# A three-step integer conversion moved from SBUF to PSUM, and slot stores that no longer wait for one another

## The chip, the cores and the metric
The kernel runs on one core of a Trainium2 chip. The number is the time of one execution in device microseconds. A core has TensorE (PE; its weight loads are shown as PEld), VectorE (DVE), ScalarE (ACT), GpSimd (POOL) and SyncE (SP), which only starts transfers here; each takes its instructions in the order of the program and waits on semaphores. SBUF is the on-chip memory, PSUM the small memory that TensorE writes and that DVE and ACT can also read and write.

## What is computed
Attention over 4 batches and 8 heads of 576 rows, in which each row keeps its 32 largest scores; then a dense two-layer network; then a layer in which each of the 2304 tokens goes to one of eight experts. The weights `w_in` and `w_out` of the dense network arrive as 64-bit floats.

```python
scores = scale * np.matmul(q, k.transpose(0, 1, 3, 2))
kth = np.partition(scores, -32, axis=-1)[..., -32:-31]
attn = softmax(np.where(scores >= kth, scores, -1e9)); x = attn @ v
h = x @ w_in                                     # 512 -> 2048
x = (np.maximum(h, 0) + alpha * np.minimum(h, 0)) @ w_out
e = argmax(x @ w_gate + modality_bias[modality_id])   # one of 8 experts
out = gate_w * (np.maximum(x @ w1[e], 0) @ w2[e])
```

## The kernel before
**The loop.** Attention runs as 72 steps of two tiles of 128 query rows. One step puts on each engine: on TensorE the scores of the next pair into the PSUM bank pair `psS` (L453, L454); on ScalarE a copy of them to SBUF (`S`, L457), a mask `u` (L526), the exponential (L530) and a 16-bit copy `HL` (L534); on GpSimd the factors `bc` (L506), the masking (L527) and the low halves of `HL` (L538, L539); on VectorE the search for the 32 largest (L471 to L501). The search begins with three instructions on `psS` and `S` (L474), and it is L471 behind them that frees `psS` for the next scores. SP then starts a transposing transfer `PT<-HL` (L541). Six steps ahead, q, k and v of a later head pair are loaded, scaled, split into 16-bit halves (`qk`, L419 on GpSimd) and transposed (`QK<-qk`, L423 on SP). All of this is one written order per engine; nothing reorders it at run time.

**The weights.** `all_weights` spreads the 32 pieces of `w_in` and `w_out` (128 x 512 64-bit words each) over the steps before 205 us. SP loads a piece into one of five buffers `wraw`. `read(x)` turns its words into 32-bit floats on DVE in three instructions: L259 shifts the high word, L260 joins the sign bits, L261 joins the top bits of the low word. In the kernel before all three write the same SBUF tile, `f32[x]`, which lies in the space of `Wi` or `Wo`, or, for the last four pieces of each matrix, in one of four tiles `wlast`. The pieces are read up to four at a time, at the end of a step, so on DVE they stand between one step's search and the next. `square` (L266, ScalarE) takes each read piece for a norm, `high` and `low` (L271 to L282) split it later; a `wlast` tile is free again only when `low` (L280 on GpSimd, L282 on DVE) has read it.

**The expert lists.** When the rank of a token within its expert is known, `place(r)` writes the token's number and weight to its slot in the DRAM table `mapD`, by an indirect transfer that GpSimd starts (L773; 18 of them from 418 to 908 us). Two stores of one chunk are declared independent; a store of the next chunk is not, so its wait includes the landing of the store before it. The list of a block (`ids<-mapD`, L1446 for block 0, L1309 for the later units) is read by SP behind the last store.

**Around block 0.** After the last attention step the loop goes on with the dense network alone: TensorE forms `psS` (L637) and then `psX` (L686), for which ScalarE makes the high part of `g` (L672) and GpSimd the low part (L673). Into that stretch falls the end of the placing: one store of the small chunk, two of chunk 7, then block 0's list.

Of the kernel before, what the change touches and what calls it, by code (L numbers as in the profile page):

```python
# [8 lines left out]
F32 = mybir.dt.float32  # L9
# [3 lines left out]
I32 = mybir.dt.int32  # L13
I64 = mybir.dt.int64
AF = mybir.ActivationFunctionType
ALU = mybir.AluOpType
# [44 lines left out]
def tile_kernel(ctx, tc, q, k, v, w_in, w_out, alpha, mod_id, w_gate, mod_bias, w1, w2, out, dbg=None, force=False):  # L61
    nc = tc.nc
    V, A, G, T, SY = nc.vector, nc.scalar, nc.gpsimd, nc.tensor, nc.sync
# [11 lines left out]
    psX = ctx.enter_context(tc.tile_pool(name="psX", bufs=2, space=PSUM))  # L75
# [4 lines left out]
    mapD = dram.tile([SLOTS, 2], I32, name="mapD")  # L80
# [78 lines left out]
    def run(exact):  # L159
        with ExitStack() as rs:  # L160
            rc = rs.enter_context(tc.tile_pool(name="rc", bufs=1))
            flags = None if exact else rc.tile([128, 2 * 144 + NFB], BF16, name="flags")
            ohs = rc.tile([128, E], F16, name="ohs")
            G.memset(ohs, 0.0)
            mp = Rec()
            with tc.manual_schedule():
                with ExitStack() as ph:
                    blk, over = phase1(exact, ph, rc, rs, flags, ohs, mp)
                mp.B = rs.enter_context(tc.tile_pool(name="moeB", bufs=1))
                if exact:  # L170
                    moe_phase(MAXBLK, blk, mp)
                else:
                    units_phase(blk, mp, lambda: doubts(rc, flags, blk, over))
            if not exact:
                return nc.values_load(blk[0:1, 32:33], min_val=0, max_val=(2 * 144 + NFB) * 128 + MAXBLK)


    def phase1(exact, ph, rc, rs, flags, ohs, mp):
# [15 lines left out]
        def at(slot, s_, f):  # L194
            hooks[slot].setdefault(s_, []).append(f)
# [34 lines left out]
        def all_weights(words, stage):  # L230

            n = 512
# [5 lines left out]
            sc, iv, raws, f32 = {}, {}, {}, {}  # L238
# [12 lines left out]
            def read(x):  # L251

                w_, i = divmod(x, 16)
                f32[x] = W[w_][:, (i + WG) * n:(i + WG + 1) * n] if i + WG < 16 else \
                    stage.tile([128, n], F32, name="wlast", bufs=WG)
                r3 = raws.pop(x).bitcast(I32).rearrange("p (n w) -> p n w", w=2)
                lo, hi = r3[:, :, 0], r3[:, :, 1]
                t_ = f32[x].bitcast(I32)
                V.tensor_scalar(t_, hi, 5, 2, op0=ALU.logical_shift_left, op1=ALU.logical_shift_right)  # L259
                V.scalar_tensor_tensor(t_, hi, -1073741824, t_, op0=ALU.bitwise_and, op1=ALU.bitwise_or)  # L260
                V.scalar_tensor_tensor(t_, lo, 29, t_, op0=ALU.logical_shift_right, op1=ALU.bitwise_or)  # L261

            def square(x):
                w_, i = divmod(x, 16)
# [331 lines left out]
        def chunk(ci, xn, rs):  # L596
            ffn = state.ffn
            c = Rec()
            R = len(rs)
# [171 lines left out]
            def place(r):  # L771
                G.memset(spacer, 0.0)
                d_ = G.indirect_dma_start(out=mapD, out_offset=bass.IndirectOffsetOnAxis(ap=c.si[:, r:r + 1], axis=0),  # L773
                                          in_=c.tg[:, r, :], in_offset=None)
                if r:
                    tc.declare_no_dep(d_.ins, c.placed.ins, reason="other slots")
                c.placed = d_
                state.placed += 1

            def keep():  # L780
# [13 lines left out]
            def after(s_):  # L794
# [28 lines left out]
                for r in range(R):  # L823
                    at("late", s_ + GATE[2] + r, lambda r=r: place(r))
# [54 lines left out]
        state = Rec()  # L879
# [6 lines left out]
        wgroup = all_weights(words, stage)  # L886
        state.ffn = state.out = None
        state.started = state.placed = 0
        state.alone = False

        def wstep(n):
# [51 lines left out]
        def first_block(s_):  # L943

            if s_ < NIT + 4:
                return at("mid", s_ + 1, lambda: first_block(s_ + 1))
            mp.A = rs.enter_context(tc.tile_pool(name="moeA", bufs=1, side="right"))
            b0 = Rec()
            cp = bankO[:, COUNTS:COUNTS + 8]
            T.matmul(cp, ones16, ohs, start=True, stop=True)  # L950
            mx = rc.tile([128, 1], F32, name="mx0")
            ge = rc.tile([128, 8], F32, name="ge0")
            ix = rc.tile([128, 1], F32, name="ix0")
            mp.oh0 = rc.tile([128, 8], F32, name="oh0")
            mp.e0 = rc.tile([128, 1], F32, name="e0")
            blk0 = rc.tile([128, 2], I32, name="blk0")


            mp.cn = rc.tile([128, 8], I32, name="cn")
            mp.cb = [rc.tile([128, 16], F32, name=f"cb{i}") for i in range(4)]  # L960
            for t_ in mp.cb:
                G.memset(t_, 0.0)
            mp.less = rc.tile([128, 8], F32, name="less")
            mp.step = rc.tile([128, 8], F32, name="step")
            mp.base = rc.tile([128, 16], F32, name="base")
            mp.ef = rc.tile([128, 16], F32, name="ef")
            mp.cx = rc.tile([128, 16], F32, name="cx")
            mp.blk = rc.tile([128, 33], I32, name="blk")
            mp.at = rc.tile([128, 8], F32, name="at8")
            mp.part = rc.tile([128, 8], I32, name="part8")  # L970
            mp.some = rc.tile([128, 8], F32, name="some8")
            mp.few = rc.tile([128, 8], F32, name="few8")
            mp.ix = rc.tile([128, 1], F32, name="ix8")
            mp.over = rc.tile([128, 1], F32, name="over")
            V.reduce_max(mx, cp, axis=AX.X)
            V.scalar_tensor_tensor(ge, cp, mx, iota8m, op0=ALU.is_ge, op1=ALU.mult)
            V.tensor_reduce(ix, ge, axis=AX.X, op=ALU.min)
            V.tensor_scalar(mp.e0, ix, 8.0, None, op0=ALU.add)
            V.tensor_copy(blk0[:, 0:1], mp.e0)
            V.tensor_scalar(blk0[:, 1:2], mp.e0, float(CAP), None, op0=ALU.mult)  # L980
            V.tensor_scalar(mp.oh0, iota8m, ix, None, op0=ALU.is_equal)

            def prepare():
                oh0 = mp.oh0
                V.tensor_scalar(mp.less, oh0, -256.0, 255.0 if exact else 0.0, op0=ALU.mult, op1=ALU.add)
                V.tensor_scalar(mp.step, oh0, -256.0, float(CAP), op0=ALU.mult, op1=ALU.add)
                V.scalar_tensor_tensor(mp.step[:, 0:7], oh0[:, 1:8], 256.0, mp.step[:, 0:7], op0=ALU.mult, op1=ALU.add)
                if exact:
                    V.tensor_scalar(mp.base, io16[:, :, 0], oh0[:, 0:1], 256.0, op0=ALU.add, op1=ALU.mult)
                else:  # L990
                    V.tensor_scalar(mp.base, io16[:, :, 0], 2.0, oh0[:, 0:1], op0=ALU.mult, op1=ALU.add)
                    V.tensor_scalar(mp.base, mp.base, 256.0, None, op0=ALU.mult)
                    V.scalar_tensor_tensor(mp.at, oh0, 256.0, ebase, op0=ALU.mult, op1=ALU.add)

            def start():
                assert state.placed == NTILE - 2
                mp.b0 = Block(0, blk0[0:1, 0:1], blk0[0:1, 1:2], mp)
                for fp in range(4):
                    mp.b0.load(fp)

            at("late", s_, start)
            at("gap", s_ + 1, prepare)
            at("late", s_ + 1, lambda: mp.b0.gather())
            for fp in range(4):
                at("gap", s_ + 2 + fp, lambda fp=fp: mp.b0.split(fp))
            at("gap", s_ + 3, lambda: mp.b0.turn())
# [48 lines left out]
        while True:  # L1055
# [69 lines left out]
            while fpq and credit >= 1 and n_ < 2 and fpq[0][0] <= s_ and weights_for(fpq[0][2]):  # L1125
                credit -= 1
                _, c, fp = fpq.pop(0)
# [173 lines left out]
    class Unit:  # L1301


        def __init__(self, i, R, ie, ip, mp):
            self.i, self.R, self.mp = i, R, mp
            self.e = SY.value_load(ie, min_val=0, max_val=E - 1)
            pos = SY.value_load(ip, min_val=0, max_val=E * CAP)
            self.ids = small.tile([128, 4, 2], I32, name="ids4")
            SY.dma_start(self.ids[:, :R], mapD[bass.ds(pos, 128 * R), :].rearrange("(p r) o -> p r o", r=R))  # L1309
            self.raw, self.wp, self.gs = {}, {}, {}  # L1310

        def gather(self):
# [82 lines left out]
    def moe_phase(nblk, blk, mp):  # L1395
# [17 lines left out]
        for i in range(1, nblk):  # L1413
# [21 lines left out]
            o.m2(3)  # L1435
            o.store()

    class Block:


        def __init__(self, i, ie, ip, mp):
            self.i, self.mp = i, mp
            self.e = SY.value_load(ie, min_val=0, max_val=E - 1)
            pos = SY.value_load(ip, min_val=0, max_val=E * CAP)
            self.ids = small.tile([128, 2, 2], I32, name="ids")
            SY.dma_start(self.ids, mapD[bass.ds(pos, 256), :].rearrange("(p r) o -> p r o", r=2))  # L1446
            self.raw, self.wp = {}, {}
            self.gs = {}
            self.Y = None
# [116 lines left out]
```

## Time and profile before
| what | value |
|---|---|
| median of three runs | 1156.09 us (1155.61 to 1158.4) |
| the profiled execution | 1153.87 us, its span 1152.2 us |
| DVE, ACT, POOL, PE busy | 823.8, 755.2, 718.0, 845.0 us |
| L259, L260, L261 | 32 each, all before 205 us |
| L773 | 18, from 418.0 to 907.8 us |

The span is the time from the first to the last instruction in the profile; the execution's own time is 1.67 us more. Line numbers (L259) are those of the kernel before. In a row of the timeline the columns are start, duration, engine, line, operation, output `<-` inputs, shape, and in brackets the idle time before it and what ended that. A wait for several semaphores is put down to the one that came last as far as the profile shows it.

### The profile page before, as it was taken

The page shows a single profiled execution, that of the slowest core. Times are in us where ns is not written, and L with a number is a line of the kernel's source. Part 1 is how long each engine was busy: PE and PEld are TensorE (multiplying, and loading weights), DVE is VectorE, ACT ScalarE, POOL GpSimd, SP SyncE. Part 2 cuts the span into 40 slices and gives each one's busy share as a digit, 9 for nine tenths or more (in the row PEclk, how much of TensorE's full clock was granted, in tenths as well). Part 3 has the DMA queues.
Part 4 walks back from the last instruction along what each step waited for, and adds up shares of the span by engine and source line. Part 5 has one row for each costly group of instructions (what it writes and reads, how often), then busy time and mean ns, then how long its engine had stood idle before and what let it go on. Part 6 is the DMA issues. An engine that isn't in the chain of part 4 may idle for free.

```text
span 1152.2 us, 21482 instructions
## 1 busy us (share of the span) xinstructions
PE 845.0 (73%) x7100; PEld 602.6 (52%) x7100; DVE 823.8 (72%) x2813; ACT 755.2 (66%) x1276; POOL 718.0 (62%) x1106
## 2 busy tenths in 40 slices
PE   0202231347869989878787878989998899999995
PEld 0001121234536557455555555667665778888884
DVE  5788878788889999999888879994326343434342
ACT  6466696898987887878888978795324243342441
POOL 4175496899898898888788999897323220230210
PEclk9999565668899999999989999999999999999998
DMA  8969965586788577586778768765104272543320
GB/s 250 251 171 237 263 145 128 137 180 162 165 202 162 107 184 126 106 177 133 147 148 172 158 138 193 155 128 79 19 19 165 86 262 75 183 135 121 129 92 22
DMA packets 297111, 170.22 MB, mean 148 GB/s; under 512 B 245458, under 2 KB 270034, under 8 KB 296988
## 3 DMA queue, kind: packets, MB, share of 16 engines
q1 hardware_dynamic: 293212, 158.24, 59.0%
q0 software_dynamic: 3776, 10.51, 2.5%
q8 instruction: 57, 0.93, 0.4%
q14 instruction: 66, 0.54, 0.2%
HBM read 81.42 MB, written 25.94 MB: 93 GB/s over the span
## 4 chain that ended last, share of the span: by engine, by line
PE 34%; DVE 23%; POOL 15%; ACT 12%; issue 7%; DMA 6%; SPq 3%; ACTq 0%; POOLq 0%
PE psX L1363 9%; PE psS L1380 9%; PE psX L686 6%; DVE X L501 4%; DVE m L477 4%; PE psS L637 4%; POOL HL L538 4%; POOL S L527 4%; DVE F L477 3%; DMA rawk<-in_k_dram 3%; ACT S L530 2%; POOL qk L419 2%; DVE gr L665 2%; ACT HL L534 2%; PE psH L637 2%
## 5 line engine op out<-in xcount | busy, mean ns | idle before, releaser
L686 PE MATMUL psX<-Wo,g 128*128 128x512 f16 x864 | 218.6, 403 | 53.8 <-POOL g L673 39.6
L527 POOL TENSOR_TENSOR S<-u,S 128x576 f32<-128x576 bf16 x144 | 184.5, 1303 | 47.4 <-ACT u L526 47.2
L637 PEld LDWEIGHTS <-Wi 128*128 128x128 f16 x1920 | 170.8, 99 | 45.7 <-DVE gr L665 14.3
L538 POOL TENSOR_TENSOR HL<-S,HL 128x512 f16<-128x512 f32 x144 | 168.2, 1168 | 20.3 <-ACT HL L534 10.5
L453 PE MATMUL psS<-QK 128*128 128x512 f16 (+1 forms) x160 | 63.7, 436 | 142.6 <-DVE B L471 109.4
L637 PE MATMUL psH<-xT,Wi 128*128 128x256 f16 (+1 forms) x1488 | 158.2, 265 | 12.3 <-DVE gr L665 8.5
L686 PEld LDWEIGHTS <-g 128*128 128x128 f16 x864 | 82.9, 103 | 157.1 <-POOL g L673 49.2
L530 ACT ACTIVATE S<-S,bc,nb 128x576 f32<-128x576 f32 x144 | 124.0, 862 | 40.7 <-POOL S L527 40.7
L453 PEld LDWEIGHTS <-QK 128*128 128x128 f16 (+1 forms) x320 | 32.1, 109 | 203.1 <-DVE B L471 59.5
L1389 POOL DMA_INDIRECT out_dram<-o,ids x18 | 19.9, 1106 | 166.8 <-ACT o L1387 164.0
L477 DVE MAX8 m<-X 128x8 f32<-128x160 f32 x432 | 117.6, 314 | 0.0
L673 POOL TENSOR_TENSOR g<-gr,g 128x512 f16<-128x512 f32 x72 | 84.0, 1166 | 52.6 <-ACT g L672 47.3
L526 ACT ACTIVATE u<-S,bc 128x576 bf16<-128x576 f32 x144 | 103.1, 765 | 15.8 <-POOL bc L506 15.8
L1370 DVE SCALAR_TENSOR_TENSOR gl<-psX,gh 128x512 fp32r<-128x512 f32 (+1 forms) x40 | 25.4, 637 | 115.5 <-ACT gh L1369 110.9
L534 ACT ACTIVATE HL<-S 128x576 f16<-128x576 f32 x144 | 91.3, 680 | 12.9 <-DMA PT<-HL 12.7
L1369 ACT ACTIVATE gh<-psX 128x512 fp32r<-128x512 f32 (+1 forms) x40 | 22.3, 557 | 109.7 <-PE psX L1363 107.9
L457 ACT ACTIVATE S<-psS 128x576 f32<-128x576 f32 x144 | 84.1, 633 | 8.6 <-PE psS L454 8.6
L501 DVE MATCH_REPLACE8 X<-m,X 128x160 f32<-128x160 f32 x288 | 87.0, 310 | 0.0
L558 PE MATMUL bankO<-VV,PT 128*128 128x66 f16 (+1 forms) x2240 | 86.0, 200 | 0.0
L558 PEld LDWEIGHTS <-PT 128*128 128x128 f16 (+1 forms) x2240 | 82.3, 105 | 4.8 <-issue 3.5
L474 DVE SCALAR_TENSOR_TENSOR X<-psS,S 128x288 f32<-128x288 f32 (+1 forms) x144 | 80.8, 603 | 2.5
L672 ACT ACTIVATE g<-gr 128x512 f16<-128x512 f32 x72 | 44.9, 623 | 40.5 <-DVE gr L665 24.1
(290 smaller groups left out, 2098.6 us busy)
## 6 DMA issues: line engine op xcount, KB each, us to landing
raw<-in_moe_w_dram SPq DMA_DIRECT2D x40, 512.0 KB
qkD<-QK SPq DMA_DIRECT2D x16, 576.0 KB
QK<-qkD SPq DMA_DIRECT2D x16, 576.0 KB
wraw<-in_moe_w_in_dram SPq DMA_DIRECT2D x16, 512.0 KB
wraw<-in_moe_w_out_dram SPq DMA_DIRECT2D x16, 512.0 KB
vvD<-VV SPq DMA_DIRECT2D x16, 325.0 KB
VV<-vvD SPq DMA_DIRECT2D x16, 325.0 KB
K<-QK SPq DMA_DIRECT2D x32, 144.0 KB
```

What stands on the lines that cost most here:

```text
L477: ops.append(lambda: V.max(o, a_))
L501: ops.append(lambda i_=i_, r=r: V.match_replace(out=dst(i_), in_to_replace=m[:, i_, 8 * r:8 * r + 8], in_values=src(i_) if r == 0 else dst ...
L526: A.activation(u, t.S, AF.Relu, scale=-BIG, bias=t.cut)
L527: G.tensor_tensor(t.S, u, t.S, op=ALU.subtract)
L530: A.activation(t.S, t.S, AF.Exp, scale=t.c.negc, bias=t.b)
L534: A.activation(t.HL.rearrange("p a b -> p (a b)")[:, 0:S], t.S, AF.Copy)
L538: G.tensor_tensor(f[:, 640:1152], t.S[:, 0:512], f[:, 0:512], op=ALU.subtract)
L558: T.matmul(oo, l, r, start=(n_ == 0), stop=(n_ == len(ops) - 1), skip_group_check=True)
L637: T.matmul(h[:, fb, :], Wi[:, 4 * cc + f0 // 512, wh, f0 % 512:f0 % 512 + 128], c.xT[:, :R, xh_, cc, :], start=(n == 0), stop=(n == 11))
L686: T.matmul(c.X2[r], g[:, gh, fb, r * 128:r * 128 + 128], Wo[:, FB * fp + fb, wh, :], start=(fp == 0 and fb == 0 and n == 0), stop=(fp == c ...
L1363: T.matmul(h, w_[:, cc, f0:f0 + 128], x_[:, cc, :], start=(n == 0), stop=(n == 11))
L1380: T.matmul(self.Y[r], g_[:, r * 128:r * 128 + 128], w_[:, j % 2, :], start=(j == 0 and n == 0), stop=(j == 7 and n == 2))
```

## The change
Three edits. The first two results of `read` go to a PSUM tile `psX` (two buffers, which the dense network uses only later); only the third is written to SBUF. Each store of `place` is declared independent of all stores before it. In return every list read names all the stores that no list has named yet (`behind`), in place of the dependence that came through the chain of stores.

```diff
-                t_ = f32[x].bitcast(I32)
+                t_ = psX.tile([128, n], F32, name="psX").bitcast(I32)
                 V.tensor_scalar(t_, hi, 5, 2, op0=ALU.logical_shift_left, op1=ALU.logical_shift_right)
                 V.scalar_tensor_tensor(t_, hi, -1073741824, t_, op0=ALU.bitwise_and, op1=ALU.bitwise_or)
-                V.scalar_tensor_tensor(t_, lo, 29, t_, op0=ALU.logical_shift_right, op1=ALU.bitwise_or)
+                V.scalar_tensor_tensor(f32[x].bitcast(I32), lo, 29, t_, op0=ALU.logical_shift_right, op1=ALU.bitwise_or)
...
-                if r:
-                    tc.declare_no_dep(d_.ins, c.placed.ins, reason="other slots")
-                c.placed = d_
+                for p_ in state.places:
+                    tc.declare_no_dep(d_.ins, p_.ins, reason="other slots")
+                state.places.append(d_)
...
+                mp.places, mp.seen = state.places, 0
+                behind(mp.b0.list, mp)
...
+    def behind(list_, mp):
+        for p_ in mp.places[mp.seen:]:
+            tc.add_manual_dep(list_.ins, p_.ins.name, mybir.DependencyInfo(
+                mybir.DependencyClass.Sync, mybir.DependencyReason.DATA), reason="all that was placed")
+        mp.seen = len(mp.places)
```

The order of instructions on every engine is the same in both kernels; what differs is the operands and the waits. On DVE, at the start of the program (`wraw` is the loaded piece, `Wi` the SBUF tile), before:

```order
L259 TENSOR_SCALAR Wi<-wraw 128x512 [waits DMAHW7_49]
L260 SCALAR_TENSOR_TENSOR Wi<-wraw,Wi 128x512 [waits DVE_49]
L261 SCALAR_TENSOR_TENSOR Wi<-wraw,Wi 128x512 [waits DVE_49]
L259 TENSOR_SCALAR Wi<-wraw 128x512 [waits DMAHW0_49]
L260 SCALAR_TENSOR_TENSOR Wi<-wraw,Wi 128x512 [waits DVE_49]
```

and after:

```order
L259 TENSOR_SCALAR psX<-wraw 128x512 [waits DMAHW7_49]
L260 SCALAR_TENSOR_TENSOR psX<-wraw,psX 128x512 [waits DVE_49]
L261 SCALAR_TENSOR_TENSOR Wi<-wraw,psX 128x512 [waits DVE_49]
L259 TENSOR_SCALAR psX<-wraw 128x512 [waits DMAHW0_49]
L260 SCALAR_TENSOR_TENSOR psX<-wraw,psX 128x512 [waits DVE_49]
```

Only the tiles are others: L260 and L261 now have one operand in PSUM and one in SBUF. On POOL, where the small chunk's store and chunk 7's two stand one behind the other (the waits named DMASW are landings of transfers that POOL started), before:

```order
L745 COPY tg<-tok 128x2 [waits DMASW4_49,DMASW3_49]
L772 MEMSET spacer 1x1
L773 DMA mapD<-tg,si 18944x2
L772 MEMSET spacer 1x1 [waits Pool_49]
L773 DMA mapD<-tg,si 18944x2 [waits DMASW5_49,DVE_49]
L772 MEMSET spacer 1x1 [waits Pool_49]
L773 DMA mapD<-tg,si 18944x2
L673 TENSOR_TENSOR g<-gr,g 128x512 [waits Activation_49]
```

and after:

```order
L745 COPY tg<-tok 128x2 [waits DMASW4_49,DMASW3_49]
L772 MEMSET spacer 1x1
L773 DMA mapD<-tg,si 18944x2
L772 MEMSET spacer 1x1 [waits Pool_49]
L773 DMA mapD<-tg,si 18944x2 [waits DVE_49]
L772 MEMSET spacer 1x1 [waits Pool_49]
L773 DMA mapD<-tg,si 18944x2
L673 TENSOR_TENSOR g<-gr,g 128x512 [waits Activation_49]
```

The wait for one landing, DMASW5, is gone from the second store; L673, which TensorE needs, stands behind all three. On SP, at block 0's list, before:

```order
L1446 DMA ids<-mapD 128x4 [waits DMAHW5_49,DMASW7_49]
```

and after (the line is L1455 there):

```order
L1455 DMA ids<-mapD 128x4 [waits DMASW5_49,DMASW4_49,DMASW6_49,DMASW3_49,DMASW7_49,DMASW2_49,DMAHW5_49,DMASW1_49,DMASW0_49]
```

The list waits for the landings of all stores by name in place of the last one's alone.

## Rows read from the trace of the kernel before
**Rows 1.** Page, part 2: busy tenths in 40 slices of 28.8 us.
```profile
DVE  5788878788889999999888879994326343434342
POOL 4175496899898898888788999897323220230210
```
**Rows 2.** Windows, 0 to 205 us, of L259, L260, L261: length, DVE busy (count).
```profile
0.00:205.00 205.00, 22.82 (x32) 0.81 0.77 204
0.00:205.00 205.00, 28.23 (x32) 0.81 0.77 204
0.00:205.00 205.00, 29.77 (x32) 0.81 0.77 204
```
**Rows 3.** Lines one by one: ns min/median/max, first and last start, shape.
```profile
L259 DVE TENSOR_SCALAR wlast<-wraw x8: 408/1370/1642, 57.4 to 191.9; 128x512 int32<-128x512 int32 x8
L260 DVE SCALAR_TENSOR_TENSOR Wi<-wraw,Wi x12: 691/693/1639, 9.8 to 56.1; 128x512 int32<-128x512 int32 x12
L474 DVE SCALAR_TENSOR_TENSOR psS<-psS,S x72: 441/453/467, 39.8 to 776.6; 128x288 f32<-128x288 f32 x72
L1370 DVE SCALAR_TENSOR_TENSOR gl<-psX,gh x40: 408/692/693, 935.0 to 1136.1; 128x512 fp32r<-128x512 f32 x32, 128x256 fp32r<-128x256 f32 x8
L212 DVE TENSOR_SCALAR sck<-bankO x16: 150/153/154, 14.7 to 653.5; 128x3 int32<-128x3 int32 x16
```
**Rows 4.** Groups by line and shape, DVE: busy us, mean ns, idle before.
```profile
L572 DVE TENSOR_SCALAR den<-bankO,sv 128x4 f32<-128x4 f32 x32 | 8.8, 276 | 5.9 <-PE bankO L558 5.9
```
**Rows 5.** Lines one by one, POOL.
```profile
L216 POOL TENSOR_SCALAR sci<-sck x16: 227/236/692, 15.3 to 659.4; 128x3 int32<-128x3 int32 x16
L419 POOL TENSOR_TENSOR qk<-rawk,qk x16: 1267/1282/1718, 19.9 to 670.1; 128x576 f16<-128x576 f32 x16
```
**Rows 6.** Timeline, 55 to 110 us, of DVE, POOL and SP.
```profile
55.61 0.41 DVE L259 TENSOR_SCALAR Wi<-wraw 128x512 int32<-128x512 int32 x1
68.10 0.46 DVE L474 SCALAR_TENSOR_TENSOR psS<-psS,S 128x288 f32<-128x288 f32 x1
...
58.13 3.23 POOL L527 TENSOR_TENSOR S<-u,S 128x576 f32<-128x576 bf16 x2 [10.82 <-ACT u L526]
...
64.64 2.47 SPq L423 DMA_TRANSPOSE QK<-qk  x1
...
98.25 0.41 DVE L259 TENSOR_SCALAR Wo<-wraw 128x512 int32<-128x512 int32 x1
109.29 0.46 DVE L474 SCALAR_TENSOR_TENSOR psS<-psS,S 128x288 f32<-128x288 f32 x1
```
**Rows 7.** Timeline, 175 to 206 us, of DVE, PE and POOL.
```profile
179.55 1.36 DVE L259 TENSOR_SCALAR wlast<-wraw 128x512 int32<-128x512 int32 x1 [3.06 <-POOL Wi L280]
193.70 0.46 DVE L474 SCALAR_TENSOR_TENSOR psS<-psS,S 128x288 f32<-128x288 f32 x1
...
196.19 0.59 PE L453 MATMUL psS<-QK 128*128 128x512 f16 x1 [22.91 <-DVE B L471]
...
201.78 0.20 POOL L506 TENSOR_TENSOR bc<-m,nb 128x4 f32<-128x4 f32 x1 [10.34 <-DVE wp1k L212]
...
204.69 2.54 POOL L527 TENSOR_TENSOR S<-u,S 128x576 f32<-128x576 bf16 x2
```
**Rows 8.** Timeline, 860 to 870 us, of POOL, PE and SP.
```profile
860.17 0.98 POOL L773 DMA_INDIRECT mapD<-tg,si  x1 [0.42 <-issue]
864.57 0.97 POOL L773 DMA_INDIRECT mapD<-tg,si  x1 [3.32 <-DVE mx L975]
865.84 0.97 POOL L773 DMA_INDIRECT mapD<-tg,si  x1 [0.22 <-issue]
866.84 1.16 POOL L673 TENSOR_TENSOR g<-gr,g 128x512 f16<-128x512 f32 x1
...
868.05 2.33 PE L686 MATMUL psX<-Wo,g 128*128 128x512 f16 x10 [3.28 <-POOL g L673]
...
869.62 0.36 SPq L1446 DMA_DIRECT2D ids<-mapD  x1
```

More of the change, by code (lines that the diff above doesn't have):

```diff
@@ L888, in phase1 @@
         state.started = state.placed = 0
+        state.places = []
         state.alone = False
@@ L1308, in __init__ @@
             self.ids = small.tile([128, 4, 2], I32, name="ids4")
-            SY.dma_start(self.ids[:, :R], mapD[bass.ds(pos, 128 * R), :].rearrange("(p r) o -> p r o", r=R))
+            behind(SY.dma_start(self.ids[:, :R], mapD[bass.ds(pos, 128 * R), :].rearrange("(p r) o -> p r o", r=R)), mp)
             self.raw, self.wp, self.gs = {}, {}, {}
@@ L1445, in __init__ @@
             self.ids = small.tile([128, 2, 2], I32, name="ids")
-            SY.dma_start(self.ids, mapD[bass.ds(pos, 256), :].rearrange("(p r) o -> p r o", r=2))
+            self.list = SY.dma_start(self.ids, mapD[bass.ds(pos, 256), :].rearrange("(p r) o -> p r o", r=2))
+            if i:
+                behind(self.list, mp)
             self.raw, self.wp = {}, {}
```

## The prediction
> **What bounds the kernel now.** I read the page's slices first. DVE and POOL are both busy in most slices up to about 800 us and both idle much of the time behind that [rows 1], so the kernel has an attention part that runs on several engines at once and an end that runs on TensorE. The change touches one place in each: the reading of the weights, all of it before 205 us, and three slot stores near 864 us. So I looked at these two stretches in the timeline.
>
> In the first stretch the three lines of `read` take 22.82 + 28.23 + 29.77 = 80.8 us of DVE for 32 pieces, 2.53 us a piece [rows 2]. Line by line the same instruction has two durations: L260 takes 0.69 us in its median case and up to 1.64 us, L259 0.41 us at best and 1.37 us in the median of its late pieces [rows 3]. The added microsecond is about one POOL instruction, and POOL is stretched in the same places: L216 takes up to 0.69 us against a median of 0.24, L419 up to 1.72 against 1.28, both at 15 to 22 us [rows 5]. The two engines hold each other up. With the short durations a piece would cost 0.41 + 0.69 + 0.69 = 1.79 us, 57.3 us in all, so 23.5 us of the 80.8 are such waiting. L474, which reads one operand from PSUM and one from SBUF and writes PSUM, stays between 441 and 467 ns in all 72 cases, although POOL is as busy around them [rows 1, 3]. That is the form which L260 gets, and L261 gets that of L1370 (PSUM and SBUF in, SBUF out), which never exceeds 0.693 us.
>
> **The reads, price of one.** L260 and L261 go to 0.69 us each, the value of L1370 for the same 512 columns. L259 in its new form (SBUF in, PSUM out) is not in the trace. Bounds: 0.41 us if it keeps its rate, and from L474, whose 288 columns take 0.45 us, to the 0.69 us of a 512-column instruction at one column a step; L212, the same double shift on int32 with PSUM as its input, has only 0.15 us of fixed cost, so nothing more is to be expected [rows 3]. I take 0.69. A piece then takes 3 x 0.69 = 2.07 us, with the small overlap seen between pieces 2.05: a piece that POOL never held gets 0.27 us longer, a held one up to 3 us shorter. In all 32 x 2.05 = 65.6 us, 15 us less DVE. That is not the gain; it counts only where DVE ends last.
>
> [...]
>
> **Where it counts.** Place by place in the order of time:
> - 9 to 22 us. Three pieces stand ahead of the first scale factors on DVE: +0.8. Against that the POOL instructions between these and the first `QK<-qk`, which goes when L419 is done, lose what they were held for: L216 0.45 and L419 0.44 [rows 5], and of the small ones in between at least one as much, together 1.3. Net -0.5; bounds +0.8 and, with two more held alike, -1.4.
> - 55 to 68 us. Four pieces take DVE from 55.61 to 68.10, 12.5 us, which become 8.2, so -4.3 on DVE. But SP sets the pace here: its `QK<-qk` at 64.64 waits for POOL, and transfers follow it back to back. POOL's L527 pair takes 3.23 us at 58.13 against 2.54 at 204.69, where no read is about, and L419 is again up to 0.44 too long [rows 5 to 7]: with a small one -1.3. I take -1.3; bounds 0 and -4.3.
> - 98 to 109 us. Four pieces, 109.29 - 98.25 = 11.0 us, become 8.2: -2.8 [rows 6]. The transfers of SP are again dense behind it, so I take a quarter, -0.7; bounds 0 and -2.8.
> - 125 to 176 us: one piece only; ScalarE is the bound. Nothing, and if that cover is gone, 0.27.
> - 176 to 202 us. Here four pieces fill DVE from 179.55 to the search at 193.70, 14.15 us, and before them it idles 3.06 us because the `wlast` tile is still being read by POOL's L280 [rows 7]. Afterwards L259 and L260 write PSUM and need not wait for it: they run from 176.5 on (179.55 less the idle 3.06), and only L261 waits until 179.55. So the first piece ends at 180.2, the other three take 6.15 and the search begins at 186.3: -7.4. What is late next? The scores (L453 at 196.19) were waiting for L471 of that search, and the factors `bc` of POOL at 201.78, idle for 10.34 us, for the search's end [rows 7]: both follow DVE in full. POOL's L419 there is needed two steps later and ends earlier than today. Bounds: -2.8 (what POOL alone is held for there) and -7.4. I take -7.4.
>
> Sum of the reads: -0.5 - 1.3 - 0.7 - 7.4 = -9.9 us. From there to 800 us every step follows from the one before and nothing hangs on absolute time, so the shift passes through.
>
> **The stores.** POOL starts the small chunk's store at 860.17, is free of it at 861.15, and starts the next store only at 864.57, 3.4 us later, 3.32 of them idle behind the small spacer instruction. The row puts that down to L975 on DVE; but the order has no such dependence: what the store takes from DVE (its slot and weight) was ready before, and the wait that goes with the change is the landing of the store before. The list of block 0 shows a landing of that size: the last store is done at 866.81, and SP, which waits for it, starts the list at 869.62, 2.8 us later. Behind the stores on POOL stands L673, and behind that TensorE, idle for 3.28 us before 868.05 [rows 8]. Without the wait the second store starts at about 861.5, the third at 862.8, L673 runs from 863.8 to 865.0 (its input from ScalarE comes before), and TensorE goes on at about 865.05: -3.0 us. Bounds 0 and -3.3. The list goes with its last landing, some 2.5 us earlier, less than TensorE gains, but block 0's first matmul stands behind four more rounds of the dense network, so that costs nothing; if it did, 0.5 us. The other stores stand some 50 us apart from the one before; their wait was over already. The list's new waits are for landings long past, except for the last, which it waited for before; SP has nothing for TensorE queued behind it but block 0's own weights.
>
> **Sum.** -9.9 - 3.0 = -12.9 us: the profiled execution's 1153.87 becomes 1141.0. The median of the runs stands 2.2 us above that execution, so 1156.09 becomes 1143.2.
>
> **The rivals.**
> - The end of the last reads does not decide (for it: ScalarE and SP are dense up to 190 us; against: the waits of L453 and L506). Then only POOL's 2.8 us count there, and none of the small terms: -2.8 - 3.0, 1150.3.
> - The store really waited for DVE, as its row says: TensorE still stalls, -9.9 alone, 1146.2. For it: the row itself, with L975 ending just before the store; against: L975 comes later in the program than the store.
> - SP is not the bound at 55 and 98 us, and DVE's full savings count: -1.4 - 4.3 - 2.8 - 7.4 - 3.0 = -18.9, 1137.2.
> - Slower: POOL holds the new forms too. The place is DVE's reads in front of the searches. These words are read at a stride of two, which L474's are not, so its steadiness need not carry over. Then each piece keeps its waiting and pays 0.27 us for the lost rate and, if PSUM has a fixed price like that of L572 (276 ns for four columns, against 153 for L212 [rows 3, 4]), 0.12 for each of three instructions: +0.63. Eighteen pieces lie where DVE sets the pace (3, 4, 3, 4, 4, the third group behind 68 us): +11.3 - 3.0, 1164.4. It decides from the point where a piece in PSUM takes longer than the 2.53 us of today.
> - The attention part absorbs all of it, and the stores' 3.0 us are all that is left: 1153.1, which is no change that can be told.
>
> **How the numbers follow.** A difference under 0.3%, 3.5 us, can't be told from none. Chances: the forecast 0.55 (its own range 1140 to 1147), the first rival 0.15, the second 0.07, the third 0.10, the slower one 0.06, absorbed 0.07. Below 1152.6 lie the forecast and the first three, 0.87, of which I give 0.02 to no change: faster 0.85, same 0.09, slower 0.06. The range 1137.5 to 1152 leaves out the slower case, the absorbed one and about half of the third.
>
> **What would show it.** L259, L260 and L261 all near 0.69 us with no case above 0.75; the search that starts at 193.70 at about 183.8; POOL's three stores following one another within 1.3 us each, and TensorE's stall before the ten L686 down from 3.28 to about 0.3 us. Wrong would be: stretched L260 or L261; an idle DVE ahead of the search near 184; the second store still 3 us behind the first.

## The result and the profile after

The changed kernel took 1142.17 us (median of 4 runs, 1141.09 to 1143.34) against 1156.03 us before (4 runs, 1155.61 to 1158.40) on the same chip: ratio 0.9876, 95% interval 0.9859 to 0.9893. 1143.2 was predicted. On a second chip the ratio was 0.9882 (0.9857 to 0.9906). The profiled execution took 1142.26 us, 11.6 less than that of before.

The two rows of slices that answer to [rows 1], and the three windows that answer to [rows 2]:

```profile
DVE  5778778688799999999888879994225333443331
POOL 3165397899988988988788999897333220230210
```

```profile
0.00:205.00 205.00, 21.92 (x32) 0.81 0.81 212
...
0.00:205.00 205.00, 22.26 (x32) 0.81 0.81 212
...
0.00:205.00 205.00, 21.98 (x32) 0.81 0.81 212
```

The slices show little: DVE is about as busy as before (806.0 us in all, it was 823.8). The windows show that the three reads now take 66.2 us where they took 80.8; 65.6 was the estimate. Line by line (ns min/median/max, first and last start, shape), against [rows 3]:

```profile
L259 DVE TENSOR_SCALAR psX<-wraw x32: 672/685/696, 9.7 to 183.4; 128x512 int32<-128x512 int32 x32
...
L260 DVE SCALAR_TENSOR_TENSOR psX<-wraw,psX x32: 695/696/697, 10.4 to 184.1; 128x512 int32<-128x512 int32 x32
...
L261 DVE SCALAR_TENSOR_TENSOR wlast<-wraw,psX x8: 686/686/689, 59.3 to 184.8; 128x512 int32<-128x512 int32 x8
```

Not one of these instructions is stretched any more; min and max are 2 to 24 ns apart. L259, which took 0.41 us at its best, now takes 0.67 to 0.70, as priced. Now the place that carried the largest term, DVE from 175 to 186 us, which answers to [rows 7]:

```profile
175.43 0.68 DVE L259 TENSOR_SCALAR psX<-wraw 128x512 int32<-128x512 int32 x1
176.14 0.69 DVE L260 SCALAR_TENSOR_TENSOR psX<-wraw,psX 128x512 int32<-128x512 int32 x1
178.57 0.69 DVE L261 SCALAR_TENSOR_TENSOR wlast<-wraw,psX 128x512 int32<-128x512 int32 x1 [1.73 <-POOL Wi L280]
...
184.81 0.69 DVE L261 SCALAR_TENSOR_TENSOR wlast<-wraw,psX 128x512 int32<-128x512 int32 x1
185.41 0.46 DVE L474 SCALAR_TENSOR_TENSOR psS<-psS,S 128x288 f32<-128x288 f32 x1
```

The search that began at 193.70 begins at 185.41. The first two reads of the first piece run in the time in which DVE idled before, and only the third, which writes `wlast`, waits for POOL. And the stores, against [rows 8]:

```profile
851.58 0.98 POOL L773 DMA_INDIRECT mapD<-tg,si  x1 [0.42 <-issue]
...
852.87 0.97 POOL L773 DMA_INDIRECT mapD<-tg,si  x1 [0.22 <-issue]
...
854.14 0.97 POOL L773 DMA_INDIRECT mapD<-tg,si  x1 [0.22 <-issue]
855.14 1.16 POOL L673 TENSOR_TENSOR g<-gr,g 128x512 f16<-128x512 f32 x1
...
856.36 2.33 PE L686 MATMUL psX<-Wo,g 128*128 128x512 f16 x10 [0.17 <-POOL g L673]
```

The three follow one another at 1.3 us, and TensorE's wait is 0.17 us in place of 3.28. From the first store to TensorE's ten products it is 4.78 us; it was 868.05 - 860.17 = 7.88.

How the shift grows is read from the starts of L474 (the searches), each time the same search before and after: 39.79 and 39.74 us (the first), 109.29 and 104.83, 125.42 and 123.21, 167.25 and 166.25 (the ninth), 193.70 and 185.41 (the tenth), 776.63 and 768.26 (the last). So 1.0 us came from all that lies ahead of the ninth search, 7.3 from the stretch behind it, nothing from there to 770 us, and 3.1 at the stores. These add up to 11.4 of the profiled 11.6. The open question was why the places ahead of the ninth search gave 1.0 and not the predicted 2.5, though the search at 109 us had been 4.5 earlier.

### The profile page after: what moved, and what is told of

Read it like the earlier page. It is cut to its first block, busy times and chain, and to the rows that moved or that the text cites. A ratio compares the mean times of both kernels' runs of the same rounds, so it can differ in the third digit from the quotient of the medians.

```text
span 1140.5 us, 21484 instructions
## 1 busy us (share of the span) xinstructions
PE 844.8 (74%) x7100; PEld 602.5 (53%) x7100; DVE 806.0 (71%) x2813; ACT 755.4 (66%) x1276; POOL 706.2 (62%) x1106
## 4 chain that ended last, share of the span: by engine, by line
PE 33%; POOL 17%; DVE 17%; ACT 16%; DMA 7%; issue 7%; SPq 2%; POOLq 0%; ACTq 0%
PE psS L1383 9%; PE psX L1366 8%; PE psX L686 6%; POOL HL L538 4%; POOL S L527 4%; PE psS L637 4%; DVE m L477 3%; DVE X L501 3%; ACT S L530 3%; DMA PT<-HL 3%; ACT HL L534 2%; ACT S L457 2%; DVE F L477 2%; DMA rawk<-in_k_dram 2%; ACT u L526 2%
## 5 line engine op out<-in xcount | busy, mean ns | idle before, releaser
L637 PE MATMUL psH<-xT,Wi 128*128 128x256 f16 (+1 forms) x1488 | 158.4, 265 | 12.4 <-DVE gr L665 8.2
L673 POOL TENSOR_TENSOR g<-gr,g 128x512 f16<-128x512 f32 x72 | 84.0, 1167 | 53.4 <-ACT g L672 47.8
L474 DVE SCALAR_TENSOR_TENSOR X<-psS,S 128x288 f32<-128x288 f32 (+1 forms) x144 | 80.7, 602 | 2.5
```

The source lines that it names most:

```text
L637: T.matmul(h[:, fb, :], Wi[:, 4 * cc + f0 // 512, wh, f0 % 512:f0 % 512 + 128], c.xT[:, :R, xh_, cc, :], start=(n == 0), stop=(n == 11))
```

## Experiments

Each was timed, in 5 to 12 runs, against the kernel before on its own chip: e1 to e4 on one, e5, e6 and a2 on a second, e7 and e8 on a third. Ratios are therefore to the kernel before.

### Either half alone

e1_reads takes the diff's first hunk, the reads, and nothing else; e2_stores takes all the others.

```diff
# e2_stores, against the changed kernel
-                t_ = psX.tile([128, n], F32, name="psX").bitcast(I32)
+                t_ = f32[x].bitcast(I32)
-                V.scalar_tensor_tensor(f32[x].bitcast(I32), lo, 29, t_, ...)
+                V.scalar_tensor_tensor(t_, lo, 29, t_, ...)
# e1_reads: only these two lines are changed in the kernel before
```

> Only the three reads of each piece of a word use PSUM; the stores and the lists stay as before. Theory: the 8.29 us by which the searches run earlier after 185 us in the changed kernel all come from the reads, and the stores' 3.1 us (the first product of the experts' stage: 8.6 us earlier before it, 11.7 after) stand by themselves: about 8.4 us under the kernel before, near 1147.6. Rival: the stores' gain exists only because the stage starts earlier or the reads' gain is lost again at the unchanged stores, so that the parts don't add: within 2 us of the kernel before, or within 2 us of the changed one.

Measured: 1147.63 us, ratio 0.9931 (0.9909 to 0.9954).

> Only the stores and the lists are changed; the reads lie in SBUF as before. Theory: the second store leaves beside the first instead of waiting for its landing, 3 us: about 3.1 us under the kernel before, near 1152.9, with the start of the experts' stage as the only place that differs. Rival: the store was waiting for VectorE (the row before names it): then nothing, near 1156.0.

Measured: 1151.99 us, ratio 0.9972 (0.9958 to 0.9987). The halves add: 0.69 and 0.28% make 0.97, with an uncertainty of about 0.27 from their two intervals; the whole was 1.24% (1.07 to 1.41) on one chip and 1.18% (0.94 to 1.43) on the other. In e2_stores nothing on DVE is changed, and the second store leaves 1.29 us behind the first:

```profile
861.25 0.99 POOL L773 DMA_INDIRECT mapD<-tg,si  x1 [0.42 <-issue]
...
862.54 0.97 POOL L773 DMA_INDIRECT mapD<-tg,si  x1 [0.22 <-issue]
```

while in e1_reads, with the old wait, the row names another line of DVE than [rows 8] does, for the same wait:

```profile
850.80 0.98 POOL L773 DMA_INDIRECT mapD<-tg,si  x1 [0.42 <-issue]
...
855.60 0.97 POOL L773 DMA_INDIRECT mapD<-tg,si  x1 [3.73 <-DVE ge L976]
```

So the wait was for the landing of the store before, the one wait that the edit took away, and not for DVE; the name in the brackets was only what happened to end just then.

### Which pieces carry the gain

```diff
# e3_last_four (e4_all_but_last_four has x < 28)
-                t_ = psX.tile([128, n], F32, name="psX").bitcast(I32)
+                t_ = (psX.tile([128, n], F32, name="psX") if x >= 28 else f32[x]).bitcast(I32)
```

> The changed kernel, but with the intermediate in PSUM for the last four of 32 pieces only (the ones read between 175 and 195 us); the other 28 are read as before. Theory: the gain of the reads sits at those four, where the searches wait for them: of 8.3 us, 7.3 stay and with the stores' 3.1 the time is about 10.4 us under the kernel before, near 1145.6. Rival: the gain is spread evenly over the pieces, then 4/32 of 8.3 = 1.0 stay and the time is near 1152.

Measured: 1145.85 us, ratio 0.9919 (0.9895 to 0.9944).

> The counterpart: the first 28 pieces by way of PSUM, the last four as before. Theory: what the first 28 give is about 1.0 us (the searches at 166 us are 1.0 earlier in the changed kernel), with the stores 4.1 under the kernel before, near 1152. Rival of an even spread: 28/32 of 8.3 = 7.3 and 3.1, near 1145.6.

Measured: 1149.86 us, ratio 0.9949 (0.9929 to 0.9969). An even spread is out: with 4 of the 32 pieces most of the gain is there. e4 came out 2 us faster than the theory said, but its interval reaches from 1147.8 to 1152.5. The two stretches, from the starts of L474 in the traces, us:

| kernel | reads of pieces 0 to 27 | of 28 to 31 | 1st to 9th search | 9th to 10th |
|---|---|---|---|---|
| before | SBUF | SBUF | 127.46 | 26.45 |
| e2_stores | SBUF | SBUF | 126.14 | 26.46 |
| e3_last_four | SBUF | PSUM | 127.77 | 19.16 |
| e5_sbuf_scratch | SBUF, own tile | SBUF, own tile | 127.80 | 25.82 |
| changed | PSUM | PSUM | 126.51 | 19.16 |
| a2_changed_again | PSUM | PSUM | 125.90 | 19.16 |
| e1_reads | PSUM | PSUM | 125.67 | 19.16 |
| e4_all_but_last_four | PSUM | SBUF | 126.08 | 26.46 |

Leaving e5 aside, to which the next section comes, the last column has two values to 0.01 us, set by the last four pieces alone: 7.3 us. The column ahead of it scatters by 1.7 us within one form; its means are 127.29 and 126.04, so 28 pieces give about 1.25 us.

### PSUM, or only another buffer?

```diff
# e5_sbuf_scratch
-                t_ = psX.tile([128, n], F32, name="psX").bitcast(I32)
+                t_ = stage.tile([128, n], F32, name="wtmp", bufs=2).bitcast(I32)
```

> The changed kernel, but the intermediate of all 32 pieces lies in a small tile of SBUF of its own (two buffers) in place of PSUM. The first two reads of a piece no longer need the buffer that GpSimd still holds, exactly as in the changed kernel; only the memory that they use is SBUF again. Theory: most of the gain at the last four pieces is that the reads don't stretch beside GpSimd (12 reads there: 14.2 us busy before, 8.3 after, so 5.9 of the 7.3) and the earlier start gives the other 1.3: here reads of 1.3 to 1.8 us stay in the trace, the stretch from the search at 166 us to the next one lasts about 25 us (26.4 before, 19.2 after), and the time is some 5 us above the changed kernel, near 1148 to 1149. Rival: the freed buffer is the cause and the reads stretched only because of where they fell: then near 1143, with about 19 us between those searches.

Measured: 1151.20 us, ratio 0.9953 (0.9936 to 0.9969), 7.4 above the changed kernel where some 5 were expected; the changed kernel on the same chip 1143.80:

> The changed kernel once more, unaltered, on the chip of the two others, as their measure: 1142.2 as before, within 0.3%. Its stretch from the search at 166 us to the next one should again last 19.2 us; the one from the first search (40 us) to that at 166 us shows how far a kernel scatters there between executions.

Its last pieces in the timeline:

```profile
176.91 0.43 DVE L259 TENSOR_SCALAR wtmp<-wraw 128x512 int32<-128x512 int32 x1
177.37 0.69 DVE L260 SCALAR_TENSOR_TENSOR wtmp<-wraw,wtmp 128x512 int32<-128x512 int32 x1
180.72 1.63 DVE L261 SCALAR_TENSOR_TENSOR wlast<-wraw,wtmp 128x512 int32<-128x512 int32 x1 [2.66 <-POOL Wi L280]
...
190.14 1.79 DVE L260 SCALAR_TENSOR_TENSOR wtmp<-wraw,wtmp 128x512 int32<-128x512 int32 x1
191.97 1.65 DVE L261 SCALAR_TENSOR_TENSOR wlast<-wraw,wtmp 128x512 int32<-128x512 int32 x1
193.54 0.45 DVE L474 SCALAR_TENSOR_TENSOR psS<-psS,S 128x288 f32<-128x288 f32 x1
```

The first two reads run ahead of the wait here too, and the time is lost again behind it: seven of the twelve reads take 1.4 to 1.8 us each. The free buffer is worth 26.45 - 25.82 = 0.6 us (1.3 was expected); the memory of the intermediate 25.82 - 19.16 = 6.7. The two were taken in this order only. With reads that no longer stretch the earlier start may be worth more: an estimated 1.4 us, the 0.68 and 0.69 that run ahead of the wait in the changed kernel; no run has the intermediate in PSUM without the free buffer. The same L261 takes up to 1.73 us with `wraw` and `wtmp`, both in SBUF, and 0.69 in all 32 cases of the changed kernel with `wraw` and `psX`. Why the one form is stretched beside POOL's instructions and the other is not, no trace shows.

### Where the upstream gain went

In the changed kernel DVE idles ahead of the words at 80 us. The row of its waits between 60 and 130 us (us in total, times, longest), and SP's queue at the same place, with the last instruction of POOL that its transposes `PT<-HL` need:

```profile
DVE psX L259 <- DMA wraw<-in_moe_w_out_dram: 9.6, 2, 6.6
```

```profile
68.27 0.30 POOL L539 TENSOR_TENSOR HL<-S,HL 128x64 f16<-128x64 f32 x1
...
62.75 2.48 SPq L423 DMA_TRANSPOSE QK<-qk  x1
65.27 0.81 SPq L123 DMA_DIRECT2D al<-in_moe_alpha_dram  x1
...
72.25 0.47 SPq L133 DMA_DIRECT2D modt<-in_moe_modality_id_dram  x1
72.84 2.73 SPq L541 DMA_TRANSPOSE PT<-HL  x2
75.66 1.97 SPq L247 DMA_DIRECT2D wraw<-in_moe_w_out_dram  x4
```

SP came only 1.9 us earlier (64.64 before [rows 6]), so the 4.1 us that DVE had gained by 64 us went into the wait. Either SP's issuing sets that pace, or what the DMA engines can carry (their share is 0.97 to 1.02 between 80 and 120 us). I held the second.

```diff
# e6_constants_late, against the changed kernel
-LCON = [("late", 1), ("late", 3), ("late", 5)]
+LCON = [("late", 6), ("late", 7), ("late", 8)]
```

> The changed kernel with one edit more: SyncE's 10 loads of constants (65 to 73 us) and 5 stores of zeros (102 to 105 us) move behind the stretch in which the words are loaded (to the slots late 6, 7 and 8 of the same table), so that every load and transpose behind them in SyncE's queue leaves 7.6 us earlier from 73 us on and 2.9 more from 105 us on. Theory for the missing part of the upstream gain (1.0 of 2.5 us came): the landings of 80 to 128 us are set by what the DMA engines carry, not by when SyncE issues: under 2 us faster than the changed kernel, 1140.5 to 1143. Rival: SyncE's queue sets the pace there, as the prediction had it: the searches at 85 to 125 us come 5 us or more earlier and the time is 1135 to 1138.

Measured: 1133.16 us, ratio 0.9791 (0.9767 to 0.9815), 10.6 under the changed kernel on the same chip. The theory fell and the rival held, with a time below even the rival's 1135 to 1138:

```profile
63.50 2.46 SPq L423 DMA_TRANSPOSE QK<-qk  x1
66.08 3.35 SPq L541 DMA_TRANSPOSE PT<-HL  x2
69.54 1.96 SPq L247 DMA_DIRECT2D wraw<-in_moe_w_out_dram  x4
```

The words leave 6.1 us earlier, the wait for them is gone from DVE's list, and the searches of 85.94, 104.83 and 123.21 start at 79.81, 98.32 and 113.57. That the DMA engines could carry more is seen in the changed kernel itself. While SP issues the small loads (11 of them, from 65.27 to 72.72; the expectation counts 10) their share falls to 0.25 (68 to 72 us). In e6 that gap is filled, and the stretch from 80 us is as full as before. The columns are the window, its length, DVE busy (count), PE clock, DMA share, GB/s:

```profile
60.00:80.00 20.00, 19.49 (x50) 1.00 0.86 234
80.00:100.00 20.00, 16.57 (x47) 0.75 1.02 255
```

The edit also takes 2.9 us of POOL's `zero`, `dummy` and `tok` from 62.65 us away; its share was not measured apart. The trace of the changed kernel bounds it: POOL is done with `HL` at 68.57, and SP comes to the transposes of it at 72.84, so an estimated 4.3 of the 6.1 us at least were SP's own. Not all of the gain lasts: at the ninth search e6 is 17.3 us ahead of the changed kernel (148.96 and 166.25), at the tenth 9.5 (175.92 and 185.41). To see what the reads are worth once SP is out of the way:

```diff
# e8_constants_late_reads_sbuf, against e6_constants_late
-                t_ = psX.tile([128, n], F32, name="psX").bitcast(I32)
+                t_ = f32[x].bitcast(I32)
```

> The kernel with the constants late, but with the three reads in SBUF as in the kernel before all changes (stores and lists changed). It tells what SyncE's queue did with the upstream gain: between the first search (40 us) and the one before the last pieces the changed reads gave 1.25 us with the constants in their old place (mean of four kernels with either form), where the prediction had 2.5. Theory: the words' loads stood behind the constants in SyncE's queue and VectorE waited 6.6 us for them at 80 us, so what the reads gained by then was spent in that wait; with the constants away the first to the eighth search take 2.5 us or more longer here than in the kernel with the constants late (108.9 us). Rival: the reads there give little in any order: under 1.5 us. The time is 1133.2 and up to 10 more: near 1141 if the last pieces cost what they did, less if GpSimd's stall there hides them.

Measured: 1144.42 us, ratio 0.9914 (0.9892 to 0.9937), where near 1141 was expected. From the first search to the one before the last pieces (the ninth; the expectation counts it as the eighth) it takes 119.69 us, and 108.87 with PSUM: 10.8 us where the old order had 1.25. The last pieces give less here than there, 31.22 - 26.96 = 4.3 us for 7.3. In the whole times the reads are worth 1.2% (0.9914 to 0.9791), and 0.9 to 1.0% in the old order (0.9972 to 0.9882 and 0.9876); their intervals do not tell these apart, so it is the stretch in the traces, one of each kernel, that shows the difference. DVE's busy time says why; the columns are those above. First e8:

```profile
60.00:80.00 20.00, 19.69 (x43) 1.00 0.82 213
80.00:100.00 20.00, 19.69 (x43) 0.98 0.94 232
```

and the changed kernel, in the old order:

```profile
60.00:80.00 20.00, 13.20 (x40) 1.00 0.59 116
80.00:100.00 20.00, 16.18 (x44) 1.00 0.97 285
```

With the constants away and the reads in SBUF DVE is full and sets the pace; with the constants in place and the reads in PSUM DVE idles a third of the first window and SP sets it. The two bounds stand close together, and in this stretch an edit of one alone is cut off by the other.

### One stall more

e6 took the last use of the constants along into the stretch of the last pieces: POOL's compare L155 now waits there for ScalarE's Abs, and behind it stands the product L280 of POOL for which DVE waits. POOL's longest wait in e6 between 146 and 200 us:

```profile
POOL flags L155 <- ACT steep L154: 8.2, 1, 8.2
```

The diff moves the Abs to the slot before:

```diff
# e7_constants_late_abs_early, against e6_constants_late
         def stores():
+            A.activation(steep, al, AF.Abs)
...
-            A.activation(steep, al, AF.Abs)
             G.tensor_scalar(flags[:, 2 * 144:], steep, 1.0, None, op0=ALU.is_gt)
```

> The kernel with the constants late, and in it ScalarE's Abs of alpha (0.2 us) issued one slot earlier than GpSimd's compare that reads it, so that it no longer stands behind ScalarE's wait for transposes. In the profile of the kernel before this edit GpSimd's compare L155 waited 8.22 us for that Abs at 163 us, and VectorE 9.36 us for GpSimd's product L280 behind it. Theory: the wait decides, as the waits on that chain did in the stretch from 176 to 194 us of the kernel before all changes: the search at 176 us comes 7 to 8 us earlier, the time is near 1126. Rival: something else of that stretch is late next (the transposes for which ScalarE waits to 164.7 us, DMA): 0 to 3 us, 1130 to 1133.

Measured: 1128.39 us, ratio 0.9780 (0.9757 to 0.9802), the fastest median here but not told apart from e6 by its interval. DVE's longest wait between 146 and 200 us, in e6 and then in e7:

```profile
DVE wlast L261 <- POOL Wi L280: 9.4, 1, 9.4
```

```profile
DVE wlast L261 <- POOL Wi L280: 5.2, 1, 5.2
```

The search behind it comes 22.74 us after the ninth in place of 26.96: 4.2 us, between theory (7 to 8) and rival (0 to 3). ScalarE's longest wait there, 3.9 us for the transposes `PT<-HL`, speaks for what the rival named as late next; no run tests that.

## Why the prediction was right, and where it was not

- **Durations.** 0.69 us for each read, in any neighbourhood: right, and the slower case (POOL holding the new forms too) is out in 96 of 96 instructions. A fixed price of PSUM, for which the slower case set 0.12 us an instruction, does not show either: L260 takes 696 ns in the median with one source in PSUM, where it took 693 with both in SBUF [rows 3].
- **176 to 202 us, -7.4.** Measured -7.3, and e3 and e4 put it on these four pieces alone; the rival in which the end of the last reads does not decide (1150.3) fell by it. In the prediction's sum 14.15 - 8.2 = 5.95 us are for shorter reads and the other 1.4 for the earlier start. In e5 the earlier start alone gave 0.6 us; the memory gave the rest.
- **9 to 22 us, -0.5.** The transposes `QK<-qk` did start 0.76 us earlier (21.65 and 20.89), but the first search starts at 39.79 and 39.74. That the gain passes on to the first search did not hold; nothing is left of it.
- **55 to 68 and 98 to 109 us, -1.3 and -0.7.** That SP and not DVE sets the pace was right, and the rival without SP (1137.2) fell by it: DVE was 4.1 and 4.5 us earlier at the two searches, SP 1.9 and 2.1, and at the ninth search 1.0 was left. But the sum over the three upstream terms was -2.5 and some -1.25 came; the mean is known to less than a microsecond only. These are the mis-sized terms: the prediction followed SP's earlier start through to the search, and did not ask for the next landings in its queue. SP is 2.1 us ahead at 117 us and 0.8 at 121, the search 2.2 ahead at 125 us and 0.8 at 139; what took it there was not tried.
- **The stores, -3.0.** Measured -3.1 in the traces, and against the row's own name for the releaser: the order of the program was the better witness, and the rival that trusted the name (1146.2) fell by e2.
- **The sum.** The traces make it 1.25 + 7.3 + 3.1 = 11.65 against 12.9 predicted and 11.6 profiled; the medians differ by 13.9 and, on the second chip, 13.5. The 11.65 lies in the second chip's interval (10.9 to 16.5 us) and just outside the first's (12.4 to 16.3). Single runs of the kernel before scatter from 1151.3 to 1164.9 (39 runs beside the experiments), and no run settles the two microseconds between. That the predicted median was met to 1.0 us is thus in part luck: the traces' sum came out 1.25 us smaller than predicted, the medians' difference 1.0 larger. By the prediction's own sign, the tenth search, it was further off: 185.41 where about 183.8 was said.

## What to carry to other kernels

Where two engines hold each other up, count the held instructions only in the stretch in which the engine that you change ends last: 4 of 32 pieces carried 7.3 of some 8.5 us. When a gain on one engine is spent in a wait for a queue, look at what that queue issues ahead of the awaited transfer: moving 5 stores and 11 small loads that nobody needed yet, with 2.9 us of POOL's set-up, gave more here (10.6 us) than the reads alone (8.4 in e1). A releaser named beside a wait is the last event before it, not a proof (L975 stood beside 3.32 us and L976 beside 3.73, which were 0.22 once the store no longer waited for a landing); read the program's order too.

## What was not expected of the hardware

L985, eight columns wide, is an instruction of 0.16 to 0.17 us in every other trace, but of before it says:

```profile
L985 DVE TENSOR_SCALAR less<-oh x1: 3042/3042/3042, 866.3 to 866.3; 128x8 f32<-128x8 f32 x1
```

It began beside POOL's third store and ended, at 869.32, with POOL's L673 (868.13 + 1.16 = 869.29). In e1_reads the same L985 began beside the same store and took 0.17 us; there it was L987, seven columns wide, that began later beside the store and ended with L673 (857.87 + 1.16 = 859.03):

```profile
866.28 3.04 DVE L985 TENSOR_SCALAR less<-oh 128x8 f32<-128x8 f32 x1
...
868.13 1.16 POOL L673 TENSOR_TENSOR g<-gr,g 128x512 f16<-128x512 f32 x1
```

```profile
856.91 0.17 DVE L985 TENSOR_SCALAR less<-oh 128x8 f32<-128x8 f32 x1
...
857.18 1.88 DVE L987 SCALAR_TENSOR_TENSOR step<-oh,step 128x7 f32<-128x7 f32 x1
857.87 1.16 POOL L673 TENSOR_TENSOR g<-gr,g 128x512 f16<-128x512 f32 x1
```

So these look like the stretched reads: a DVE instruction that ends with one of POOL's or shortly behind it (in the trace of before the read L260 of 188.52 us ended at 190.31, POOL's L419 at 189.77), here one of a few columns that lasts microseconds. What held them beside the store, in the 0.56 and 0.69 us before L673 began, was not tried.
